# Second MLP over blocks of 512, 512, 512, 512 and 256 tokens in place of six blocks of 384

## The chip, the cores and the metric

The kernel runs on one core of a Trainium2 chip. The metric is the device time of one execution in microseconds (us); before the change it is 930.15 us, the median of three runs (930.00 to 930.42).

## What is computed

A sparse attention feeds two MLPs. With 2,304 tokens, 512 features and 2,048 hidden units, all in float32:

```
attn = softmax(mask(q @ k.T / 8)) @ v          # 4 batches, 8 heads, 576 positions
x  = attn as [2304, 512]
x2 = relu(x @ w1_in)**2 @ w1_out               # first MLP
h  = x2 @ w2_in                                # second MLP
y  = (h * sigmoid(1.702 * h)) @ w2_out
```

The weights arrive as float64 and are rebuilt as float32 on the chip ("decode").

## The kernel before

Every float32 product is made of three fp32r products: each operand is split into a high part and a low part (names ending in h and l), and high x high, low x high and high x low are summed in one PSUM bank.

The second MLP goes over the tokens in six blocks of 384, and within a block over 16 slices f of 128 hidden units. One such step, a **pass**, consists of

- `mm_h` (L340): 12 matmuls of 128x384, four input slices times three products, into one of the two banks tagged `h`. The weights are the stationary operand and the tokens (`xh`, `xl`) the moving one, so a matmul is as wide as the block.
- `act_sig`: ScalarE takes the sigmoid (L368), VectorE multiplies by h (L369), ScalarE rounds to the high part `gh` (L370), VectorE subtracts to get the low part `gl` (L371). Each of these is as wide as the block.
- `mm_acc2` (L395), called by `second`: for each token tile of 128 the stationary operand is a slice of `gh` or `gl` and the moving one is the output weights, 512 wide. With three token tiles there are nine matmuls of 128x512, three in each of three banks tagged `acc`. There are four such banks; the next block takes the next three in turn. A bank is summed over all 16 passes of its block and is then copied to SBUF and stored (`store_out`, L513).

The tokens of the next block are read back from DRAM (`load_x2`, L496 to L499) into a part of the ring `xh`, `xl` that holds 1,152 tokens. While the last block of the first MLP and the first block of the second run, VectorE and ScalarE still decode the weights of the second MLP: for each half slice VectorE does two TENSOR_SCALAR (L112, L114), two SCALAR_TENSOR_TENSOR (L119, L123) and one subtraction (L131), and ScalarE two operations (L110, L129).

The first MLP has blocks of 512, 256 and four times 384 tokens. Its `mm_h` is the same function; its second product, `mm_acc1` (L380), has the weights as stationary operand and `gh`, `gl` moving, so there both kinds of matmul are as wide as the block. Attention matmuls (L202, L223, L277, L301) are worked in between.

The order on each engine is set by a scheduler that simulates a timeline, except that TensorE's order in the first MLP and in the very last pass is that of the code.

Of the kernel before, what the change touches and what calls it, by code (L numbers as in the profile page):

```python
# [8 lines left out]
F32 = mybir.dt.float32  # L9
# [3 lines left out]
AF = mybir.ActivationFunctionType  # L13
ALU = mybir.AluOpType
# [7 lines left out]
def kernel(  # L22
# [20 lines left out]
    nc = tc.nc  # L43
    B, H, S, D = q.shape
    NT, DM = out.shape
    DFF = w1_in.shape[1]
    P = 128
    KC = DM // P
    NF = DFF // P

    NB2, NBMAX = 384, 512
    CUT1, CUT2 = [0, NBMAX, *range(768, NT + 1, 384)], [*range(0, NT + 1, NB2)]
    BLOCKS = [[(t0, t1 - t0) for t0, t1 in zip(cut, cut[1:])] for cut in (CUT1, CUT2)]
    N1, N2 = len(BLOCKS[0]), len(BLOCKS[1])
    RING = 2 * S
# [14 lines left out]
    def bank(tag):  # L70
        bufs = {"acc": 4, "h": 2, "att": 2}[tag]
        return psum.tile([P, 512], F32, tag=tag, name=f"ps_{tag}", bufs=bufs)

    xh = cpool.tile([P, KC, RING], F32R, name="xh")
    xl = cpool.tile([P, KC, RING], F32R, name="xl")
    x2d = dram.tile([P, KC, NT], F32, name="x2d")

    def f32(ap):
        return ap.bitcast(F32)
# [5 lines left out]
    marks = [None, None]  # L85
# [63 lines left out]
    def idle(ps, n):  # L149
        for _ in range(n):  # L150
            nc.tensor.matmul(ps, zeros[0][:, 0:P], zeros[0], start=True, stop=True)
# [175 lines left out]

    def mm_h(m, i, f, ph, ks, xl_last=False):
        ih, il = w_t[m, f][0:2]
        t0, nb = BLOCKS[m][i]  # L330
        c0 = t0 % RING
        prods = [(kk, w, x) for kk in ks for w, x in ((ih, xh), (il, xh), (ih, xl))]
        if xl_last:
            prods.sort(key=lambda p: p[2] is xl)
            idle(bank("h"), 4)
        for kk, w, x in prods:
            if xl_last and x is xl:
                idle(bank("h"), 3)
                xl_last = False
            nc.tensor.matmul(  # L340
                ph[:, 0:nb], w[:, kk * P:(kk + 1) * P], x[:, kk, c0:c0 + nb],
                start=(kk == KS[0] and w is ih and x is xh), stop=(kk == KS[-1] and x is xl),
            )
# [3 lines left out]
    def act_tiles(nb):  # L347
        return (
            gpool.tile([P, NBMAX], dt, tag=tag, name=tag, bufs=bufs)[:, 0:nb]
            for tag, dt, bufs in (("t", F32, 1), ("gh", F32R, 2), ("gl", F32R, 2))  # L350
        )
# [11 lines left out]
        nc.vector.tensor_tensor(out=gl, in0=t, in1=f32(gh), op=ALU.subtract)  # L363
        return gh, gl

    def act_sig(ph):
        t, gh, gl = act_tiles(NB2)
        marks[0] = nc.scalar.activation(t, ph[:, 0:NB2], AF.Sigmoid, scale=1.702)  # L368
        nc.vector.tensor_tensor(out=t, in0=ph[:, 0:NB2], in1=t, op=ALU.mult)  # L369
        marks[1] = nc.scalar.copy(gh, t)  # L370
        nc.vector.tensor_tensor(out=gl, in0=t, in1=f32(gh), op=ALU.subtract)  # L371
        return gh, gl
# [15 lines left out]
    def mm_acc2(f, g, acc, ts):  # L388
        _, _, oh, ol = w_t[1, f]
        gh, gl = g  # L390
        for lo, tt in ts:
            for t in tt:
                sl = slice(t * P, (t + 1) * P)
                for x, w in ((gl, oh),) if lo else ((gh, oh), (gh, ol)):
                    nc.tensor.matmul(  # L395
                        acc[t], x[:, sl], w,
                        start=(f == 0 and w is oh and not lo), stop=(f == NF - 1 and lo == 1),
                    )
# [81 lines left out]
    for word in FRONT.split():  # L480
        step, _, z = word.partition("+")
# [10 lines left out]
        fetch(0, n)  # L492

    def load_x2(i, c):
        s = lpool.tile([P, DM], F32, tag="tmp", name="tmp", bufs=6)[:, 0:NB2]
        nc.sync.dma_start(s, x2d[:, c, i * NB2:(i + 1) * NB2])  # L496
        c0 = i * NB2 % RING
        nc.scalar.copy(xh[:, c, c0:c0 + NB2], s)
        nc.vector.tensor_tensor(  # L499
            out=xl[:, c, c0:c0 + NB2], in0=s, in1=f32(xh[:, c, c0:c0 + NB2]), op=ALU.subtract,  # L500
        )

    def spill_x2(i, acc):
        pool, bufs = (lpool, 6) if lpool else (apool, 3)
        t0, nb = BLOCKS[0][i]
        for c in range(KC):
            s = pool.tile([P, DM], F32, tag="tmp", name="tmp", bufs=bufs)[:, 0:nb]
            (nc.scalar.copy if c % 2 else nc.vector.tensor_copy)(s, acc[c][:, 0:nb])  # L508
            nc.sync.dma_start(x2d[:, c, t0:t0 + nb], s)

    def store_out(i, t, acc):
        s = lpool.tile([P, DM], F32, tag="tmp", name="tmp", bufs=6)
        (nc.scalar.copy if t % 2 else nc.vector.tensor_copy)(s, acc)  # L513
        nc.sync.dma_start(out[i * NB2 + t * P:i * NB2 + (t + 1) * P, :], s)

    accs, gs = {}, {}

    def second(m, i, f):

        if f == 0:  # L520
            accs[m, i] = [bank("acc") for _ in range((KC, NB2 // P)[m])]
        acc, g = accs[m, i], gs.pop((m, i, f))
        if m == 0:
            mm_acc1(i, f, g, acc)
            if f == NF - 1:
                spill_x2(i, accs.pop((m, i)))
        elif i < N2 - 1 or f < NF - 1:
            mm_acc2(f, g, acc, [(0, range(3)), (1, range(3))])
            if f == NF - 1:
                for t in range(3):  # L530
                    store_out(i, t, acc[t])
        else:

            mm_acc2(f, g, acc, [(0, (0, 1)), (1, (0,))])
            store_out(i, 0, acc[0])
            mm_acc2(f, g, acc, [(1, (1,))])
            store_out(i, 1, acc[1])
            mm_acc2(f, g, acc, [(0, (2,)), (1, (2,))])
            for c0, copy, queue in ((0, nc.vector.tensor_copy, nc.sync), (DM // 2, nc.scalar.copy, nc.scalar)):
                s = lpool.tile([P, DM], F32, tag="tmp", name="tmp", bufs=6)[:, 0:DM // 2]  # L540
                copy(s, acc[2][:, c0:c0 + DM // 2])
                queue.dma_start(out[NT - P:NT, c0:c0 + DM // 2], s)

    gi = NPRO
# [3 lines left out]
    for i in range(N1):  # L548
        for f in range(NF):
            if i == N1 - 1 and f == 0:  # L550
                order.close()
                att.close()
                lpool = ctx.enter_context(tc.tile_pool(name="lpool", bufs=1, side="right", reuse_waits="tile"))
# [17 lines left out]
            if i == 0 and f == 0:  # L571
                ph = ph0.pop()
                mm_h(0, i, f, ph, KS[2:4], True)
            else:
                ph = bank("h")
# [23 lines left out]
    for i in range(N2):  # L599
        for f in range(NF):  # L600
            if i == 0:
                if f < 2:
                    fetch(1, 2 * (NF - 2 + f))
                    fetch(1, 2 * (NF - 2 + f) + 1)
                need(1, max(2 * f + 4, int(1.2 * (f + NF))), lpool, 6)
            if i == N2 - 1 and f == NF - 1:
                order.enter_context(tc.manual_schedule(engines={mybir.EngineType.PE}))
            ph = bank("h")
            mm_h(1, i, f, ph, KS)
            gs[1, i, f] = act_sig(ph)  # L610
            second(*prev)
            prev = (1, i, f)
            if 8 <= f < 8 + KC and i + 1 < N2:
                load_x2(i + 1, f - 8)
# [47 lines left out]
```

## Time and profile before

| | |
|---|---|
| median of three runs | 930.15 us |
| the profiled execution | 933.04 us, of it a span of 931.3 us on the core |
| TensorE matmul (PE) | 915.7 us busy, 98% of the span, 5739 matmuls |
| TensorE weight load (PEld) | 827.6 us, 89% |
| VectorE (DVE) | 491.1 us, 53% |
| ScalarE (ACT) | 410.1 us, 44% |
| granted TensorE clock | 0.995 of full speed over the span |

Matmuls overlap: the busy time of one runs past the start of the next, so what a matmul costs in a row is read from the distance between starts, not from its own duration.

### The profile page before, as it was taken

To read this page: it belongs to the slowest core of one execution; us is meant where nothing else is said; L and a number is where in the kernel's file an instruction comes from. 1 tells how busy PE (TensorE), PEld (TensorE's weight loads), DVE (VectorE), ACT (ScalarE), POOL (GpSimd) and SP (SyncE) were. 2 spreads that over 40 slices of the span, in tenths; PEclk is the share of its full clock that TensorE was granted. 3 is DMA by queue.
4 is the path that set the end of the run, shared out by engine and by line. 5 is a ranking of instruction groups with operands and counts; after the bars stand their busy time and mean duration, and the time that the engine had idled before them with its cause. 6 is when DMAs were issued, how large, how long until landed. Compare 5 with 4: busy or idle time off the path is not lost.

```text
span 931.3 us, 15027 instructions
## 1 busy us (share of the span) xinstructions
PE 915.7 (98%) x5739; PEld 827.6 (89%) x5739; DVE 491.1 (53%) x1335; ACT 410.1 (44%) x1123; POOL 2.9 (0%) x12
## 2 busy tenths in 40 slices
PE   8999999999999999999999999999999999999998
PEld 4677778899999999999999988899899999999897
DVE  4999996535563554532399998322322422322322
ACT  6977777425554544432355655322322322322222
POOL 0000000000000000000000000000000000000000
PEclk8999999999999999999999999999999999999999
DMA  8994111202210220100189501200200200100000
GB/s 203 325 343 134 32 32 33 72 1 61 62 44 14 85 63 12 36 1 1 59 268 299 198 11 34 69 1 0 68 1 1 69 1 1 60 1 1 34 1 34
DMA packets 72972, 64.34 MB, mean 69 GB/s; under 512 B 36708, under 2 KB 66116, under 8 KB 72900
## 3 DMA queue, kind: packets, MB, share of 16 engines
q1 hardware_dynamic: 72756, 63.25, 22.2%
q8 instruction: 45, 0.74, 0.3%
q14 instruction: 27, 0.22, 0.1%
q10 hardware_dynamic: 144, 0.13, 0.0%
HBM read 53.92 MB, written 9.44 MB: 68 GB/s over the span
## 4 chain that ended last, share of the span: by engine, by line
PE 85%; DVE 9%; ACT 2%; DMA 2%; issue 1%; SPq 0%; ACTq 0%; DVEq 0%
PE ps_h L340 39%; PE ps_acc L380 20%; PE ps_acc L395 19%; PE ps_h L301 2%; PE ps_att L223 2%; PE ps_att L202 1%; DVE tmp L119 1%; DVE whl L131 1%; PE ps_att L277 1%; DVE tmp L123 1%; DVE pr L239 1%; ACT pr L253 1%; DMA ld<-in_k_dram 1%; DVE pr L265 1%; DVE tmp L112 1%
## 5 line engine op out<-in xcount | busy, mean ns | idle before, releaser
L340 PE MATMUL ps_h<-xh,whl 128*128 128x384 f32 (+2 forms) x1528 | 394.8, 338 | 4.0 <-DVE whl L131 2.1
L340 PEld LDWEIGHTS ps_h<-xh,whl 128*128 128x128 f32 x1528 | 272.9, 188 | 19.1 <-DVE whl L131 2.7
L340 PE MATMUL ps_h<-xl,whl 128*128 128x384 f32 (+2 forms) x764 | 256.6, 336 | 0.0
L380 PE MATMUL ps_acc<-gh,whl 128*128 128x384 f32 (+2 forms) x768 | 153.1, 340 | 0.5 <-ACT tmp L508 0.5
L369 DVE TENSOR_TENSOR t<-ps_h,t 128x384 f32<-128x384 f32 x96 | 53.3, 556 | 187.7 <-ACT t L368 187.6
L395 PE MATMUL ps_acc<-whl,gh 128*128 128x512 f32 x576 | 150.7, 394 | 0.1
L340 PEld LDWEIGHTS ps_h<-xl,whl 128*128 128x128 f32 x764 | 143.7, 188 | 5.8
L368 ACT ACTIVATE t<-ps_h 128x384 f32<-128x384 f32 x96 | 47.2, 492 | 202.3 <-PE ps_h L340 192.4
L380 PEld LDWEIGHTS ps_acc<-gh,whl 128*128 128x128 f32 x768 | 128.3, 189 | 5.2 <-ACT tmp L508 0.7
L395 PEld LDWEIGHTS ps_acc<-whl,gh 128*128 128x128 f32 x576 | 106.6, 188 | 16.8 <-ACT tmp L508 0.5
L356 ACT ACTIVATE t<-ps_h 128x384 f32<-128x384 f32 (+2 forms) x95 | 46.1, 486 | 140.2 <-PE ps_h L340 132.8
L253 ACT ACTIVATE pr<-pr,st 72x72 f32<-72x72 f32 (+1 forms) x224 | 81.0, 365 | 23.3 <-DVE st L239 23.3
L362 DVE TENSOR_TENSOR t<-t 128x384 f32<-128x384 f32 (+1 forms) x80 | 42.3, 528 | 86.5 <-ACT gh L361 86.3
L395 PE MATMUL ps_acc<-whl,gl 128*128 128x512 f32 x288 | 83.7, 393 | 0.0
L380 PE MATMUL ps_acc<-gl,whl 128*128 128x384 f32 (+2 forms) x384 | 82.1, 335 | 0.0
L371 DVE TENSOR_TENSOR gl<-t,gh 128x384 fp32r<-128x384 f32 x96 | 53.4, 556 | 44.5 <-ACT gh L370 43.0
L370 ACT CAST gh<-t 128x384 fp32r<-128x384 f32 x96 | 49.2, 513 | 54.7 <-DVE t L369 53.1
L380 PEld LDWEIGHTS ps_acc<-gl,whl 128*128 128x128 f32 x384 | 66.1, 188 | 2.6
L395 PEld LDWEIGHTS ps_acc<-whl,gl 128*128 128x128 f32 x288 | 54.1, 188 | 12.5
L363 DVE TENSOR_TENSOR gl<-t,gh 128x384 fp32r<-128x384 f32 (+2 forms) x96 | 53.3, 556 | 8.8 <-ACT gh L359 4.4
L129 ACT CAST whl<-tmp 128x512 fp32r<-128x512 f32 x64 | 39.6, 620 | 16.4 <-DVE tmp L123 13.5
L110 ACT ACTIVATE tmp<-stg 128x512 f32<-128x512 f32 x64 | 42.8, 672 | 4.0 <-DMA stg<-in_moe_w_out_dram 1.9
(67 smaller groups left out, 720.8 us busy)
## 6 DMA issues: line engine op xcount, KB each, us to landing
stg<-in_moe_w_in_dram SPq DMA_DIRECT2D x32, 512.0 KB
stg<-in_moe_w_out_dram SPq DMA_DIRECT2D x32, 512.0 KB
tmp<-x2d SPq DMA_DIRECT2D x24, 192.0 KB
out_dram<-tmp SPq DMA_DIRECT2D x17, 256.0 KB
x2d<-tmp SPq DMA_DIRECT2D x16, 192.0 KB
ld<-in_k_dram SPq DMA_DIRECT2D x20, 128.0 KB
ldv<-in_v_dram SPq DMA_DIRECT2D x20, 128.0 KB
ld<-in_q_dram SPq DMA_DIRECT2D x16, 144.0 KB
```

The costliest lines, as they stand in the source:

```text
L110: nc.scalar.activation(t, high.bitcast(F32), AF.Abs)
L253: nc.scalar.activation(pr[0:R, i, j, 0:N], pr[0:R, i, j, 0:N], AF.Exp, bias=st[0:R, 0, x:x + 1], scale=-1.0, accum_out=st[0:R, 1, x:x + 1],)
L340: nc.tensor.matmul(ph[:, 0:nb], w[:, kk * P:(kk + 1) * P], x[:, kk, c0:c0 + nb], start=(kk == KS[0] and w is ih and x is xh), stop=(kk == ...
L356: marks[0] = nc.scalar.activation(t, ph[:, 0:nb], AF.Relu)
L362: nc.vector.tensor_tensor(out=t, in0=t, in1=t, op=ALU.mult)
L363: nc.vector.tensor_tensor(out=gl, in0=t, in1=f32(gh), op=ALU.subtract)
L368: marks[0] = nc.scalar.activation(t, ph[:, 0:NB2], AF.Sigmoid, scale=1.702)
L369: nc.vector.tensor_tensor(out=t, in0=ph[:, 0:NB2], in1=t, op=ALU.mult)
L370: marks[1] = nc.scalar.copy(gh, t)
L371: nc.vector.tensor_tensor(out=gl, in0=t, in1=f32(gh), op=ALU.subtract)
L380: nc.tensor.matmul(acc[c][:, 0:nb], w[:, c * P:(c + 1) * P], x, start=(f == 0 and w is oh and not lo), stop=(f == NF - 1 and lo == 1),)
L395: nc.tensor.matmul(acc[t], x[:, sl], w, start=(f == 0 and w is oh and not lo), stop=(f == NF - 1 and lo == 1),)
```

## The change

Block boundaries of the second MLP become 0, 512, 1024, 1536, 2048 and 2304. `mm_h` and `act_sig` take the width of their block, a block of 512 has four accumulators and the last one two, and the tokens of block i lie in the ring at 0 or 512 by turns. The last pass of the last block finishes its token tiles one after the other. The core of the diff:

```diff
-    NB2, NBMAX = 384, 512
-    CUT1, CUT2 = [0, NBMAX, *range(768, NT + 1, 384)], [*range(0, NT + 1, NB2)]
+    NBMAX = 512
+    CUT1, CUT2 = [0, NBMAX, *range(768, NT + 1, 384)], [*range(0, NT, NBMAX), NT]
...
     def mm_h(m, i, f, ph, ks, xl_last=False):
         ih, il = w_t[m, f][0:2]
-        t0, nb = BLOCKS[m][i]
-        c0 = t0 % RING
+        nb = BLOCKS[m][i][1]
+        c0 = i % 2 * NBMAX if m else BLOCKS[0][i][0] % RING
...
-    def act_sig(ph):
-        t, gh, gl = act_tiles(NB2)
-        marks[0] = nc.scalar.activation(t, ph[:, 0:NB2], AF.Sigmoid, scale=1.702)
-        nc.vector.tensor_tensor(out=t, in0=ph[:, 0:NB2], in1=t, op=ALU.mult)
+    def act_sig(ph, i):
+        nb = BLOCKS[1][i][1]
+        t, gh, gl = act_tiles(nb)
+        marks[0] = nc.scalar.activation(t, ph[:, 0:nb], AF.Sigmoid, scale=1.702)
+        nc.vector.tensor_tensor(out=t, in0=ph[:, 0:nb], in1=t, op=ALU.mult)
...
-            accs[m, i] = [bank("acc") for _ in range((KC, NB2 // P)[m])]
+            accs[m, i] = [bank("acc") for _ in range(BLOCKS[1][i][1] // P if m else KC)]
...
-            mm_acc2(f, g, acc, [(0, range(3)), (1, range(3))])
+            mm_acc2(f, g, acc, [(lo, range(len(acc))) for lo in range(2)])
             if f == NF - 1:
-                for t in range(3):
+                for t in range(len(acc)):
                     store_out(i, t, acc[t])
         else:
 
-            mm_acc2(f, g, acc, [(0, (0, 1)), (1, (0,))])
-            store_out(i, 0, acc[0])
-            mm_acc2(f, g, acc, [(1, (1,))])
-            store_out(i, 1, acc[1])
-            mm_acc2(f, g, acc, [(0, (2,)), (1, (2,))])
+            end = len(acc) - 1
+            mm_acc2(f, g, acc, [(lo, range(end)) for lo in range(2)])
+            for t in range(end):
+                store_out(i, t, acc[t])
+            mm_acc2(f, g, acc, [(0, (end,)), (1, (end,))])
```

`load_x2` and `store_out` use the block's own start and width in the same way. In the changed file the lines move: `mm_h` is L341 there and `mm_acc2` L397.

TensorE, inside a block. Before, from one group of nine accumulating matmuls to the next (gh is the high part, gl the low part of the activations):

```order
L395 MATMUL ps_acc<-whl,gh 128x512 x6
L395 MATMUL ps_acc<-whl,gl 128x512 x3
L340 MATMUL ps_h<-xl,whl 128x384
L340 MATMUL ps_h<-xh,whl 128x384 x2
L340 MATMUL ps_h<-xl,whl 128x384
L340 MATMUL ps_h<-xh,whl 128x384 x2
L340 MATMUL ps_h<-xl,whl 128x384
L340 MATMUL ps_h<-xh,whl 128x384 x2
L340 MATMUL ps_h<-xl,whl 128x384
L340 MATMUL ps_h<-xh,whl 128x384 x2
```

The same place inside a block of 512 now:

```order
L397 MATMUL ps_acc<-whl,gh 128x512 x8
L397 MATMUL ps_acc<-whl,gl 128x512 x4
L341 MATMUL ps_h<-xl,whl 128x512
L341 MATMUL ps_h<-xh,whl 128x512 x2
L341 MATMUL ps_h<-xl,whl 128x512
L341 MATMUL ps_h<-xh,whl 128x512 x2
L341 MATMUL ps_h<-xl,whl 128x512
L341 MATMUL ps_h<-xh,whl 128x512 x2
L341 MATMUL ps_h<-xl,whl 128x512
L341 MATMUL ps_h<-xh,whl 128x512 x2
```

Nine and twelve matmuls of two widths became twelve and twelve of one width.

TensorE, from block 0 to block 1, with buffer numbers. The accumulators of block 0 are ps_acc_6086 to 6089, those of block 1 ps_acc_6738 to 6741, in the same four banks. Now:

```order
L397 MATMUL ps_acc_6089<-whl_6507,gl_6657 128x512
L341 MATMUL ps_h_6718<-xl_73,whl_5414 128x512
L341 MATMUL ps_h_6718<-xh_72,whl_5414 128x512 x2
L341 MATMUL ps_h_6718<-xl_73,whl_5414 128x512
...
L341 MATMUL ps_h_6754<-xl_73,whl_5504 128x512
L397 MATMUL ps_acc_6738<-whl_5369,gh_6688 128x512 x2
L397 MATMUL ps_acc_6739<-whl_5369,gh_6688 128x512 x2
```

Between the last matmul into block 0's banks and the first into block 1's stand the last 7 matmuls of one `mm_h` (ps_h_6718) and all 12 of the next (ps_h_6754), 19 in all. Before, with one bank to spare, the first accumulating matmuls of block 1 stood closer and in two parts:

```order
L395 MATMUL ps_acc_6088<-whl_6476,gl_6614 128x512
L340 MATMUL ps_h_6666<-xh_72,whl_5414 128x384 x2
L340 MATMUL ps_h_6666<-xl_73,whl_5414 128x384
...
L340 MATMUL ps_h_6698<-xh_72,whl_5504 128x384 x2
L395 MATMUL ps_acc_6686<-whl_5369,gh_6642 128x512 x2
L340 MATMUL ps_h_6698<-xl_73,whl_5504 128x384
L395 MATMUL ps_acc_6686<-whl_5369,gl_6643 128x512
```

TensorE, the end of the program. Before:

```order
L340 MATMUL ps_h<-xl,whl 128x384
L395 MATMUL ps_acc<-whl,gh 128x512 x6
L395 MATMUL ps_acc<-whl,gl 128x512 x3
L395 MATMUL ps_acc<-whl,gh 128x512 x4
L395 MATMUL ps_acc<-whl,gl 128x512 x2
L395 MATMUL ps_acc<-whl,gh 128x512 x2
L395 MATMUL ps_acc<-whl,gl 128x512
```

And now:

```order
L341 MATMUL ps_h<-xl,whl 128x256
L397 MATMUL ps_acc<-whl,gh 128x512 x4
L397 MATMUL ps_acc<-whl,gl 128x512 x2
L397 MATMUL ps_acc<-whl,gh 128x512 x2
L397 MATMUL ps_acc<-whl,gl 128x512
L397 MATMUL ps_acc<-whl,gh 128x512 x2
L397 MATMUL ps_acc<-whl,gl 128x512
```

Between the last `mm_h` matmul and the first matmul on its own activations stand six matmuls where there were nine.

## Rows read from the trace of the kernel before

**Rows 1.** The page, busy time: us (share of the span) x instructions.
```profile
PE 915.7 (98%) x5739; PEld 827.6 (89%) x5739; DVE 491.1 (53%) x1335; ACT 410.1 (44%) x1123; POOL 2.9 (0%) x12
```

**Rows 2.** The page, the chain that ended last, share by line.
```profile
PE ps_h L340 39%; PE ps_acc L380 20%; PE ps_acc L395 19%; PE ps_h L301 2%; PE ps_att L223 2%; PE ps_att L202 1%; DVE tmp L119 1%; DVE whl L131 1%; PE ps_att L277 1%; DVE tmp L123 1%; DVE pr L239 1%; ACT pr L253 1%; DMA ld<-in_k_dram 1%; DVE pr L265 1%; DVE tmp L112 1%
```

**Rows 3.** Windows: length, busy PE, PEld, DVE, ACT, POOL (instructions), clock, DMA share, GB/s.
```profile
545.00:575.00 30.00, 29.85 (x150) 26.66 (x148) 30.00 (x62) 17.15 (x33) 0.00 (x0) 1.00 0.11 29
650.00:700.00 50.00, 50.00 (x252) 45.33 (x252) 16.54 (x30) 14.30 (x29) 0.00 (x0) 1.00 0.10 32
```

**Rows 4.** Timeline of TensorE, second MLP: start, duration (us), instructions, x count.
```profile
681.23 1.55 PE L395 MATMUL ps_acc<-whl,gh 128*128 128x512 f32 x6
...
708.43 0.33 PE L340 MATMUL ps_h<-xl,whl 128*128 128x384 f32 x1
...
709.50 0.33 PE L340 MATMUL ps_h<-xl,whl 128*128 128x384 f32 x1
...
710.54 1.55 PE L395 MATMUL ps_acc<-whl,gh 128*128 128x512 f32 x6
...
815.22 1.55 PE L395 MATMUL ps_acc<-whl,gh 128*128 128x512 f32 x6
```

**Rows 5.** Timeline of TensorE, first MLP, block of 512, twelve matmuls apart.
```profile
90.19 0.39 PE L340 MATMUL ps_h<-xl,whl 128*128 128x512 f32 x1
...
92.91 1.07 PE L380 MATMUL ps_acc<-gl,whl 128*128 128x512 f32 x4
```

**Rows 6.** Timeline of TensorE, first MLP, blocks of 384 and 256, twelve matmuls apart.
```profile
520.67 1.55 PE L380 MATMUL ps_acc<-gh,whl 128*128 128x384 f32 x8
...
522.75 0.51 PE L340 MATMUL ps_h<-xh,whl 128*128 128x384 f32 x2
...
178.81 1.12 PE L380 MATMUL ps_acc<-gh,whl 128*128 128x256 f32 x8
...
180.25 0.40 PE L340 MATMUL ps_h<-xh,whl 128*128 128x256 f32 x2
```

**Rows 7.** Timeline of TensorE, block of 512, right behind 16 attention matmuls.
```profile
95.15 0.40 PE L340 MATMUL ps_h<-xl,whl 128*128 128x512 f32 x1
...
96.08 0.61 PE L340 MATMUL ps_h<-xh,whl 128*128 128x512 f32 x2
```

**Rows 8.** Timeline of TensorE, first block of the second MLP; idle before and releaser in brackets.
```profile
535.34 0.86 PE L395 MATMUL ps_acc<-whl,gl 128*128 128x512 f32 x3
536.90 0.61 PE L340 MATMUL ps_h<-xh,whl 128*128 128x384 f32 x2 [0.70 <-DVE t L369]
```

**Rows 9.** Waits from 525 to 580 us: who for whom, us, times, longest.
```profile
PEld ps_h L340 <- DVE t L369: 2.3, 3, 1.1
```

**Rows 10.** VectorE's groups by shape, whole span: count | busy us, mean ns | idle before.
```profile
L371 DVE TENSOR_TENSOR gl<-t,gh 128x384 fp32r<-128x384 f32 x96 | 53.4, 556 | 44.5 <-ACT gh L370 43.0 <-PE ps_acc L395 1.1
...
L119 DVE SCALAR_TENSOR_TENSOR tmp<-stg,tmp 128x512 int32<-128x512 int32 x64 | 43.7, 685 | 0.6
...
L112 DVE TENSOR_SCALAR tmp<-tmp 128x512 f32<-128x512 f32 x64 | 26.8, 419 | 5.4 <-ACT tmp L110 5.1
...
L513 DVE COPY tmp<-ps_acc 128x512 f32<-128x512 f32 x11 | 7.1, 686 | 4.7 <-PE ps_acc L395 4.7
L363 DVE TENSOR_TENSOR gl<-t,gh 128x256 fp32r<-128x256 f32 x16 | 6.8, 425 | 1.3
```

**Rows 11.** ScalarE's groups by shape, whole span, columns as before.
```profile
L361 ACT ACTIVATE gh<-t 128x256 fp32r<-128x256 f32 x16 | 6.7, 419 | 0.4
...
L356 ACT ACTIVATE t<-ps_h 128x256 f32<-128x256 f32 x16 | 6.1, 380 | 25.6 <-PE ps_h L340 23.7 <-DVE gl L363 2.0
```

**Rows 12.** Timeline of all engines at the end.
```profile
922.48 0.35 PE L340 MATMUL ps_h<-xl,whl 128*128 128x384 f32 x1
...
922.87 0.49 ACT L368 ACTIVATE t<-ps_h 128x384 f32<-128x384 f32 x1 [2.56 <-PE ps_h L340]
...
924.75 1.09 PE L395 MATMUL ps_acc<-whl,gh 128*128 128x512 f32 x4
```

More of the change, by code (lines that the diff above doesn't have):

```diff
@@ L494, in load_x2 @@
     def load_x2(i, c):
[L495 to L498, printed above, removed]
+        t0, nb = BLOCKS[1][i]
+        s = lpool.tile([P, DM], F32, tag="tmp", name="tmp", bufs=6)[:, 0:nb]
+        nc.sync.dma_start(s, x2d[:, c, t0:t0 + nb])
+        c0 = i % 2 * NBMAX
+        nc.scalar.copy(xh[:, c, c0:c0 + nb], s)
         nc.vector.tensor_tensor(
-            out=xl[:, c, c0:c0 + NB2], in0=s, in1=f32(xh[:, c, c0:c0 + NB2]), op=ALU.subtract,
+            out=xl[:, c, c0:c0 + nb], in0=s, in1=f32(xh[:, c, c0:c0 + nb]), op=ALU.subtract,
         )
@@ L513, in store_out @@
         (nc.scalar.copy if t % 2 else nc.vector.tensor_copy)(s, acc)
-        nc.sync.dma_start(out[i * NB2 + t * P:i * NB2 + (t + 1) * P, :], s)
+        t0 = BLOCKS[1][i][0] + t * P
+        nc.sync.dma_start(out[t0:t0 + P, :], s)
     accs, gs = {}, {}
@@ L527, in second @@
         elif i < N2 - 1 or f < NF - 1:
-            mm_acc2(f, g, acc, [(0, range(3)), (1, range(3))])
+            mm_acc2(f, g, acc, [(lo, range(len(acc))) for lo in range(2)])
             if f == NF - 1:
-                for t in range(3):
+                for t in range(len(acc)):
                     store_out(i, t, acc[t])
         else:
-            mm_acc2(f, g, acc, [(0, (0, 1)), (1, (0,))])
-            store_out(i, 0, acc[0])
-            mm_acc2(f, g, acc, [(1, (1,))])
-            store_out(i, 1, acc[1])
-            mm_acc2(f, g, acc, [(0, (2,)), (1, (2,))])
+            end = len(acc) - 1
[3 more added lines that the diff above has]
+            mm_acc2(f, g, acc, [(0, (end,)), (1, (end,))])
             for c0, copy, queue in ((0, nc.vector.tensor_copy, nc.sync), (DM // 2, nc.scalar.copy, nc.scalar)):
                 s = lpool.tile([P, DM], F32, tag="tmp", name="tmp", bufs=6)[:, 0:DM // 2]
-                copy(s, acc[2][:, c0:c0 + DM // 2])
+                copy(s, acc[end][:, c0:c0 + DM // 2])
                 queue.dma_start(out[NT - P:NT, c0:c0 + DM // 2], s)
@@ L609 @@
             mm_h(1, i, f, ph, KS)
-            gs[1, i, f] = act_sig(ph)
+            gs[1, i, f] = act_sig(ph, i)
             second(*prev)
```

## The prediction

> **What bounds the kernel now.** I read the busy times first: TensorE is busy 98% of the span, VectorE 53%, ScalarE 44% [rows 1]. Busy time of overlapping matmuls proves little, so next the chain that ended last: its large pieces are the matmuls of `mm_h`, `mm_acc1` and `mm_acc2` (39, 20 and 19%), and nothing else has more than 2% [rows 2]. The windows then show what kind of bound it is: from 650 to 700 us TensorE works without a gap at the full clock, with VectorE and ScalarE at a third, while from 545 to 575 us, where weights are still decoded, VectorE is busy 30.00 of 30 us [rows 3]. So in the second MLP the time is the number of matmuls times their pace, and only near its start can another engine matter. A change that leaves the multiplications alone, as this one does, can gain only through the pace or through waits.
>
> **The pace.** It has to be read between starts. In the first MLP, long after the last change of shape, twelve matmuls take 2.72 us at 512 columns [rows 5], 2.08 us at 384 and 1.44 us at 256 [rows 6]: 226.7, 173.3 and 120.0 ns each. The steps from 256 to 384 and from 384 to 512 are both 53.3 ns for 128 columns, which leaves 13.3 ns per matmul that does not depend on its width. I call these the settled paces.
>
> The second MLP is slower than that. Equal places two blocks, 32 passes, apart lie at 681.23 and 815.22 us [rows 4], which is 4.187 us a pass (block borders included); at settled paces it would be 12 x 173.3 + 9 x 226.7 = 4,120 ns. The missing 67 ns lie behind the change of width: the first six `mm_h` matmuls behind a group of nine take 1.07 us, the six after them 1.04, which is settled [rows 4], and the nine take what is left, 4.187 - 2.11 = 2.08 us or 231 ns each. The same happens in the first MLP behind the narrow attention matmuls: four matmuls of 512 in 0.93 us, 232 ns each [rows 7], against 226.7 elsewhere in that block [rows 5]. There the two kinds of matmul are of one width, alternate just as often and use the same fresh `gh` and `gl`, yet stay settled. I take it that a change of width disturbs the pace for some ten matmuls and that this is the 67 ns.
>
> **The change part by part.**
>
> *Passes.* Before: 96 x 4.187 = 402.0 us. After: 64 passes of 24 matmuls of one width, 64 x 24 x 226.7 ns = 348.2 us, and 16 passes with 12 matmuls of 256 and 6 of 512, 16 x (1.440 + 1.360) = 44.8 us. In those 16 the width still changes. No row shows the cost of going between 256 and 512; it is bounded by nothing and by the 67 ns of a pass now, and since six of the nine wide matmuls remain I take 30 ns, 0.5 us together. So 393.5 us, a gain of 8.5 us. Of this 192 x 13.3 ns = 2.6 us come from the 192 `mm_h` matmuls that go away (960 in place of 1,152, with the same columns in all) and 5.9 from the width that no longer changes.
>
> The Trainium skill, page "TensorE: Matmul & The Clock Gate", section "Wait — 56ns, not 53.3ns?", gives a warm matmul N/2.4 + about 2.5 ns, of which only the 2.5 ns are per matmul. By that the 192 matmuls would be worth 0.5 us in place of 2.6. The rows have 13.3 ns at three widths [rows 5, 6], and the sum goes by them.
>
> *Waits while weights are decoded.* In the first block `mm_h` waits for a bank that VectorE has not yet read: three matmuls from 535.34 to 536.90 us take 1.56 us where 0.69 is usual, a loss of 0.87 [rows 8], and all weight loads waited 2.3 us in three places for this [rows 9], which bounds the loss from above because a matmul still runs meanwhile. A half slice costs VectorE 3 x 0.685 + 2 x 0.419 = 2.89 us (L119, its like L123 and L131; L112, its like L114) [rows 10]. The code asks for 1.2 halves a pass, 3.47 us, and `act_sig` adds 2 x 0.556 [rows 10]: 4.58 us in a pass of 4.19, or 109%. At 512 an operation is like the 512-wide copy, 0.686 [rows 10], so 3.47 + 1.37 = 4.84 in a pass of 5.44, or 89%. VectorE gets slack, but how the waits fall in its new order I cannot time. I take half of the loss between 0.87 and 2.3, a gain of 0.8 us; the ends are a gain of 2.3, and a loss of 2.1 if each of the three waits grows by one more decode operation of 0.685.
>
> *Block borders.* Four accumulators in four banks leave none free: the first matmul of a block must wait until the bank of the block before it is copied. It now stands 19 `mm_h` matmuls behind the last one of the old block (shown with the change), 19 x 226.7 ns = 4.3 us. Four copies of at most 0.686 [rows 10], two on VectorE and two on ScalarE, need 1.4 us. The cost is nothing. Without that cover it would be up to 1.4 us at each of four borders, 5.5 us; queued behind the copies are only the next `act_sig` and tokens for a later block.
>
> *Activations.* Inside a block of 512 they take at most 4 x 0.686 = 2.7 us [rows 10] and have 12 + 12 matmuls and more, over 5.4 us. In the block of 256: 0.380 + 0.425 + 0.419 + 0.425 = 1.65 us [rows 10, 11] against 6 + 12 matmuls, 2.8 us. Nothing is lost. The loads of tokens move the same bytes, and their buffer is free a block ahead.
>
> *The end.* The last `mm_h` matmul starts at 922.48, the sigmoid 0.39 later, and the first matmul on the result at 924.75, 1.88 behind the sigmoid [rows 12]; until then nine matmuls (2.08 us) fill the time, just enough. Now six do, 1.36 us and 0.12 for the `mm_h` matmul itself: 1.48. The chain shrinks too, to some 0.33 before the sigmoid (the 256-wide matmul is shorter) and 0.380 + 0.425 + 0.419 [rows 10, 11] plus the 0.3 us that hand-overs and the weight load take now (1.88 less operations of 0.49, 0.56 and 0.51): 1.85. A loss of 0.35 us, between nothing and 0.6. The stores behind it stay.
>
> *Sum.* -8.5 - 0.8 + 0.35 = -8.95 us. The profiled execution took 933.04, which gives 924.1. The median of the runs shown is 2.89 us below that execution, so the prediction is 930.15 - 8.95 = 921.2 us. With the ends of the terms (0.5 either way on the passes) it lies between 919.1 and 924.4.
>
> **The rivals.**
>
> *The slow pace does not come from the width.* It could belong to `mm_acc2` itself, whose stationary operand, unlike anywhere else, is `gh` and `gl`. For this speaks that the nine show no sign of settling within their group (231 ns on average), against it rows 7, where the weights are stationary and the pace suffers as well. If 67 ns a pass stayed, the passes would take 64 x 5.507 + 16 x 2.867 = 398.3, a gain of 3.7 and with the rest 4.15: 926.0 us. If all matmuls of 512 took 231 ns, 64 x 5.54 + 16 x 2.83 = 399.8: a gain of 2.2, with the rest 2.65, so 927.5 us.
>
> *Nothing changes.* If a matmul cost time by columns alone, the same columns would give the same time; then only the other terms remain and with them 929.7 us. The equal steps of 53.3 ns with 13.3 left over speak against it [rows 5, 6].
>
> *Slower: the banks.* The page "Perfetto Trace Analysis" of the Trainium skill, section "Matmuls" under "Optimizing Tensor Performance", wants independent groups to rotate through different banks, so that copying one overlaps the matmuls of the next; here that rotation ends. In this kernel the mechanism would be a copy that comes late on a queue. The wait starts when copies end more than 4.3 us behind the last matmul. At four borders and at the start of the second MLP, five in all, it outweighs the gain of 8.95 from 1.8 us each, that is with copies ending some 6.1 us behind; at 3 us each the time would be 936 us. Only decode work could delay them so, and it is over by the end of block 0; at the later borders VectorE and ScalarE are two thirds idle [rows 3]. For it speaks only the start of the second MLP.
>
> **How the numbers follow.** The settled pace for the blocks of 512 gets 0.67; the pace that stays slow 0.19 (926.0 to 927.5); no change 0.06; slower through late copies or the full VectorE queue 0.08. A difference of 0.2%, 1.9 us, is about what a measurement of this kernel can tell from none. The first two cases are faster by more than that, so faster 0.85, same 0.07, slower 0.08. The likeliest case has 919.1 to 924.4; to leave out no more than two in ten the range goes on into the second case: 918.8 to 926.8.
>
> **What would show it.** In the timeline, starts 0.227 us apart through whole passes of 512, with no slow matmuls behind the change from `mm_acc2` to `mm_h`, and places 16 passes apart in neighbouring blocks 87.0 us apart. TensorE's matmuls should fall by 192, to 5,547. The waits of `mm_h` for L369's successor should sum to less than 2.3 us, no wait of accumulating matmuls for the copies of `store_out` should appear, and one gap of a third of a microsecond before the last six matmuls. It is wrong if matmuls of 512 stay at 231 ns without a change of width, if each border shows a gap, or if VectorE falls behind through the whole first block.

## The result and the profile after

The changed kernel takes 919.71 us, the median of four runs (919.52 to 920.34). The kernel before, run beside it, took 930.28. The ratio is 0.9888 with a 95% interval of 0.9873 to 0.9902: 10.6 us less, where the forecast was 8.95 less and 921.2 us.

The page of after, busy time and the chain that ended last, beside [rows 1, 2]:

```profile
PE 904.4 (99%) x5539; PEld 792.5 (86%) x5547; DVE 486.3 (53%) x1297; ACT 404.8 (44%) x1089; POOL 2.9 (0%) x12
PE ps_h L341 42%; PE ps_acc L397 21%; PE ps_acc L382 20%; PE ps_h L302 2%; PE ps_att L224 2%; DMA stg<-in_moe_w_out_dram 2%; PE ps_att L203 2%; PE ps_att L278 1%; DMA stg<-in_moe_w_in_dram 1%; ACT pr L254 1%; PE ps_att L152 1%; DVE tmp L120 0%; DVE pr L240 0%; DVE whl L132 0%; PE ps_acc L224 0%
```

Weight loads went from 5739 to 5547, the 192 that the change takes away (eight matmul records are missing). The decode operations of VectorE (tmp L120 and whl L132), which had 1% each in [rows 2], are now at 0%: the chain runs through them less.

Three windows of after, columns as in [rows 3]:

```profile
545.00:575.00 30.00, 30.00 (x134) 24.85 (x133) 27.24 (x51) 15.06 (x27) 0.00 (x0) 1.00 0.12 36
650.00:700.00 50.00, 50.00 (x222) 41.39 (x222) 13.75 (x20) 12.06 (x20) 0.00 (x0) 1.00 0.01 5
```

While weights are decoded VectorE was busy 30.00 of 30 us; now it is 27.24, or 91%. In the 50 us from 650 TensorE works without a gap as it did, on 222 matmuls, all 512 wide, in place of 252 of two widths; the pace itself is read from starts.

The waits of before from 520 to 600 us hold, beside the row of [rows 9], one more of a weight load, at the start of the second MLP: the third accumulator of block 0 waits for ScalarE's copy (L508) out of a bank of the first MLP.

```profile
PEld ps_acc L395 <- ACT tmp L508: 0.5, 1, 0.5
```

In after no weight load waits in that time.

TensorE's timeline in after, from the first block's border to one block later:

```profile
611.29 0.39 PE L341 MATMUL ps_h<-xl,whl 128*128 128x512 f32 x1
...
615.37 0.39 PE L341 MATMUL ps_h<-xl,whl 128*128 128x512 f32 x1
615.60 1.98 PE L397 MATMUL ps_acc<-whl,gh 128*128 128x512 f32 x8
617.41 1.07 PE L397 MATMUL ps_acc<-whl,gl 128*128 128x512 f32 x4
618.32 0.62 PE L341 MATMUL ps_h<-xh,whl 128*128 128x512 f32 x2
...
702.64 1.98 PE L397 MATMUL ps_acc<-whl,gh 128*128 128x512 f32 x8
704.45 1.07 PE L397 MATMUL ps_acc<-whl,gl 128*128 128x512 f32 x4
705.36 0.62 PE L341 MATMUL ps_h<-xh,whl 128*128 128x512 f32 x2
```

Twelve accumulating matmuls take 615.60 to 618.32 = 2.72 us, 226.7 ns each, from the first one on. Sixteen passes, 615.60 to 702.64, take 87.04 us, 5.440 each: 24 x 226.7 ns and nothing else. Ahead of 615.60 stand the 19 `mm_h` matmuls at the border (611.29 to 615.60 = 4.31 us), and no row there has a bracket that names a copy.

A pass in the block of 256 (after, TensorE's timeline), where the width still changes:

```profile
894.39 1.09 PE L397 MATMUL ps_acc<-whl,gh 128*128 128x512 f32 x4
895.32 0.62 PE L397 MATMUL ps_acc<-whl,gl 128*128 128x512 f32 x2
895.78 0.40 PE L341 MATMUL ps_h<-xh,whl 128*128 128x256 f32 x2
```

Six accumulating matmuls take 1.39 us against 1.36 settled: 30 ns lost there. The narrow ones give some of it back (the order puts 18 of them behind this group), and a whole pass loses 18 to 20 ns, where the forecast had 30.

The end (after, timeline of all engines), beside [rows 12]:

```profile
910.95 1.09 PE L397 MATMUL ps_acc<-whl,gh 128*128 128x512 f32 x4
911.15 0.38 ACT L370 ACTIVATE t<-ps_h 128x256 f32<-128x256 f32 x1 [1.54 <-PE ps_h L341]
911.57 0.42 DVE L371 TENSOR_TENSOR t<-ps_h,t 128x256 f32<-128x256 f32 x1 [1.49 <-ACT t L370]
...
911.88 0.62 PE L397 MATMUL ps_acc<-whl,gl 128*128 128x512 f32 x2
912.03 0.41 ACT L372 CAST gh<-t 128x256 fp32r<-128x256 f32 x1 [0.49 <-DVE t L371]
...
912.49 0.30 PEld L397 LDWEIGHTS ps_acc<-whl,gh 128*128 128x128 f32 x2 [0.41 <-ACT gh L372]
912.49 0.73 PE L397 MATMUL ps_acc<-whl,gh 128*128 128x512 f32 x2
```

The six matmuls that fill the time last from 910.95 to about 912.3; the weight load for the last six waits until 912.49 for the rounding that began at 912.03. It stands idle for 0.41 us; since weight loads run ahead of matmuls, TensorE itself loses about 0.25. From the last matmul to the end of the span 4.14 us pass, where before had 4.68.

The profiled executions differ more, 933.04 against 919.69. Of those 13.35 us, 2.6 arise ahead of the MLPs, where the diff changes nothing, so they are no gain of the change: the first matmul of the first MLP into a bank `h` stands at 53.71 us before and 51.11 after. A window of before, then of after, shows one thing that differs there:

```profile
18.20:25.10 6.90, 6.62 (x43) 4.24 (x44) 3.45 (x8) 4.33 (x20) 0.00 (x0) 0.51 0.87 186
```

```profile
9.80:13.20 3.40, 3.18 (x14) 1.84 (x13) 0.00 (x0) 1.51 (x10) 0.00 (x0) 0.51 1.11 253
```

The granted clock stood at half, the 1.2 GHz level, for 6.9 us in one profiled execution and 3.4 in the other. TensorE had been busy 6.43 of 8.20 us ahead of it in the one and 3.36 of 4.80 in the other. I therefore compare from the first to the last matmul of `mm_acc2`: 528.99 to 926.59 = 397.60 us before, 528.56 to 913.76 = 385.20 after, 12.40 shorter. Of this 36 x 53.3 ns = 1.92 are not saved: the first three passes' `mm_h` matmuls, now wider, stand ahead of that stretch. That leaves 10.5 us, the size of the median's gain. The time from the first to the last matmul of `mm_acc2` is called its stretch below; what a run loses or gains elsewhere is not in it.

### The profile page after: what moved, and what is told of

Same layout as the page of the kernel before. It is cut to its first block, busy times and chain, and to the rows that moved or that the text cites. A ratio compares the mean times of both kernels' runs of the same rounds, so it can differ in the third digit from the quotient of the medians.

```text
span 917.9 us, 14535 instructions
## 1 busy us (share of the span) xinstructions
PE 904.4 (99%) x5539; PEld 792.5 (86%) x5547; DVE 486.3 (53%) x1297; ACT 404.8 (44%) x1089; POOL 2.9 (0%) x12
## 4 chain that ended last, share of the span: by engine, by line
PE 92%; DMA 3%; DVE 2%; ACT 2%; SPq 0%; issue 0%; ACTq 0%
PE ps_h L341 42%; PE ps_acc L397 21%; PE ps_acc L382 20%; PE ps_h L302 2%; PE ps_att L224 2%; DMA stg<-in_moe_w_out_dram 2%; PE ps_att L203 2%; PE ps_att L278 1%; DMA stg<-in_moe_w_in_dram 1%; ACT pr L254 1%; PE ps_att L152 1%; DVE tmp L120 0%; DVE pr L240 0%; DVE whl L132 0%; PE ps_acc L224 0%
## 5 line engine op out<-in xcount | busy, mean ns | idle before, releaser
L341 PE MATMUL ps_h<-xh,whl 128*128 128x512 f32 (+2 forms) x1400 | 378.6, 352 | 3.0 <-DVE whl L132 2.0
L341 PEld LDWEIGHTS ps_h<-xh,whl 128*128 128x128 f32 x1400 | 250.3, 188 | 32.7 <-DVE whl L132 2.7
L341 PE MATMUL ps_h<-xl,whl 128*128 128x512 f32 (+2 forms) x700 | 245.0, 350 | 0.0
L371 DVE TENSOR_TENSOR t<-ps_h,t 128x512 f32<-128x512 f32 (+1 forms) x80 | 51.0, 638 | 188.9 <-ACT t L370 188.9
L397 PE MATMUL ps_acc<-whl,gh 128*128 128x512 f32 x576 | 144.4, 390 | 0.0
L341 PEld LDWEIGHTS ps_h<-xl,whl 128*128 128x128 f32 x700 | 131.9, 188 | 12.6
L370 ACT ACTIVATE t<-ps_h 128x512 f32<-128x512 f32 (+1 forms) x80 | 44.4, 556 | 205.9 <-PE ps_h L341 197.9
L397 PEld LDWEIGHTS ps_acc<-whl,gh 128*128 128x128 f32 x576 | 107.0, 188 | 21.6 <-ACT gh L372 0.4
L397 PE MATMUL ps_acc<-whl,gl 128*128 128x512 f32 x288 | 78.6, 389 | 0.0
L373 DVE TENSOR_TENSOR gl<-t,gh 128x512 fp32r<-128x512 f32 (+1 forms) x80 | 51.1, 638 | 41.9 <-ACT gh L372 39.3
L372 ACT CAST gh<-t 128x512 fp32r<-128x512 f32 (+1 forms) x80 | 46.4, 580 | 48.8 <-DVE t L371 47.1
L397 PEld LDWEIGHTS ps_acc<-whl,gl 128*128 128x128 f32 x288 | 53.8, 188 | 11.3 <-DVE gl L373 0.2
L132 DVE TENSOR_TENSOR whl<-tmp,whl 128x512 fp32r<-128x512 f32 x64 | 43.9, 687 | 1.6 <-ACT whl L130 1.1
```

The lines of the kernel that those rows point to most:

```text
L132: nc.vector.tensor_tensor(out=lo, in0=t, in1=f32(hi), op=ALU.subtract)
L341: nc.tensor.matmul(ph[:, 0:nb], w[:, kk * P:(kk + 1) * P], x[:, kk, c0:c0 + nb], start=(kk == KS[0] and w is ih and x is xh), stop=(kk == ...
L370: marks[0] = nc.scalar.activation(t, ph[:, 0:nb], AF.Sigmoid, scale=1.702)
L371: nc.vector.tensor_tensor(out=t, in0=ph[:, 0:nb], in1=t, op=ALU.mult)
L397: nc.tensor.matmul(acc[t], x[:, sl], w, start=(f == 0 and w is oh and not lo), stop=(f == NF - 1 and lo == 1),)
```

## Experiments

The questions were whether the 67 ns a pass come from the change of width, as I held, or from `mm_acc2` and its stationary operand (the main rival); whether a matmul has 13.3 ns that do not depend on its width; what the waits in the first block are worth; and whether the borders cost nothing because the 19 matmuls cover the copies. The ratios are to the kernel before, run beside each group (930.69 us for E1 to E8, 931.33 for E9 to E11, 930.28 for the changed kernel itself), and as it moved by a microsecond between these groups, medians of different groups compare no better than that. Where no kernel is named, the edit is to the changed kernel.

### E1: `mm_h` 384 wide in blocks of 512

```diff
-        nb = BLOCKS[m][i][1]
+        nb = min(BLOCKS[m][i][1], 384) if m else BLOCKS[m][i][1]
...
-                sl = slice(t * P, (t + 1) * P)
+                sl = slice(t % 3 * P, (t % 3 + 1) * P)
```

`act_sig` gets the same width.

> The changed kernel, but in its blocks of 512 the first product computes 384 of the 512 token columns, the activations likewise, and the fourth token tile of the second product repeats the first one's activations: 128 tokens of each such block are left out. The number of matmuls stays (12 and 12 a pass), the two widths differ again. By columns and 13.3 ns a matmul a pass falls from 5.440 to 4.800 us, 64 of them by 41.0 us, to 878.7 us. Theory (a change of width disturbs the pace): each of these passes also loses 67 to 77 ns, 4.3 to 4.9 us together, so 883.0 to 883.6 us, with matmuls of 512 at about 231 ns. Rival (the slow pace belonged to the narrower second product with its high and low activations as stationary operand, or to three banks in place of four): the matmuls of 512 stay at 226.7 ns and the time is 878.7 us.

Measured: 883.29 us (881.80 to 884.32), ratio 0.9488 [0.9475, 0.9501]. The timeline of E1, TensorE, one pass:

```profile
701.78 2.01 PE L397 MATMUL ps_acc<-whl,gh 128*128 128x512 f32 x8
703.63 1.07 PE L397 MATMUL ps_acc<-whl,gl 128*128 128x512 f32 x4
704.54 0.33 PE L341 MATMUL ps_h<-xh,whl 128*128 128x384 f32 x1
...
706.65 2.01 PE L397 MATMUL ps_acc<-whl,gh 128*128 128x512 f32 x8
```

The same twelve accumulating matmuls now need 2.76 us instead of 2.72, and the pass 4.87 where settled paces give 12 x 173.3 + 12 x 226.7 ns = 4.80. With the change of width some 70 ns a pass come back (66 in the mean of such groups). The edit also lets the fourth token tile read the first one's activations and leaves out 128 tokens a block; the time lies where the change of width alone puts it.

### E2: every 512-wide `mm_h` matmul cut in two of 256

```diff
+            halves = (0, 256) if m and nb == NBMAX else (0,)
+            for a in halves:
+                e = a + nb // len(halves)
...
-                ph[:, 0:nb], w[:, kk * P:(kk + 1) * P], x[:, kk, c0:c0 + nb],
+                    ph[:, a:e], w[:, kk * P:(kk + 1) * P], x[:, kk, c0 + a:c0 + e],
```

> The changed kernel, with every matmul of 512 columns of the second MLP's first product cut in two of 256, same columns and weights: 768 matmuls more. Theory of 13.3 ns a matmul: 10.2 us, and 64 passes in which the width now changes between 256 and 512 at 18 to 30 ns each, 1.2 to 1.9 us: 931.1 to 931.8 us. Rival (about 2.5 ns a matmul, all else by columns): 1.9 us and the same change of width, 922.8 to 923.5 us.

Measured: 932.55 us (929.84 to 933.52), ratio 1.0015 [1.0005, 1.0025], which is 12.8 us above the median of the changed kernel, for 768 more matmuls with the same columns. The stretch of `mm_acc2`, with 732 of them, is 396.23 us long, 11.0 more than in after, so about 1.2 of the 12.8 lie outside it or between the groups of runs. One pass in E2's timeline of TensorE:

```profile
702.57 2.00 PE L400 MATMUL ps_acc<-whl,gh 128*128 128x512 f32 x8
704.41 1.07 PE L400 MATMUL ps_acc<-whl,gl 128*128 128x512 f32 x4
705.32 0.64 PE L344 MATMUL ps_h<-xh,whl 128*128 128x256 f32 x4
...
708.19 1.55 PE L400 MATMUL ps_acc<-whl,gh 128*128 128x512 f32 x6
```

Start to start it is 5.62 us against 5.440: 12 x 13.3 = 160 ns for the added matmuls and 20 for the change of width. The 24 of 256 take 2.87 us, 119.6 ns each, the pace of [rows 6]. The Trainium skill, page "TensorE: Matmul & The Clock Gate", section "Wait — 56ns, not 53.3ns?", has 2.5 ns per matmul; by an estimate from that the run would have ended at most 923.5. The measurement decides for 13.3 in this kernel.

### E5, E9: half as many changes of width in the kernel before

E9 lets blocks 1 to 5 of the kernel before run two `mm_h`, then two `mm_acc2` (nine and nine matmuls). That needs TensorE's order as in the code; E5 does this alone and is the control.

```diff
-            if i == N2 - 1 and f == NF - 1:
+            if i == 1 and f == 0:
                 order.enter_context(tc.manual_schedule(engines={mybir.EngineType.PE}))
```

> Control for the next kernel: the kernel before, with TensorE's order in the second MLP from its second block on as the code has it (12 matmuls of the first product, then the nine of the pass before). The change of width comes as often as before, so both theories expect the time of the kernel before, 930.3 us within 0.5.

Measured: 930.78 us (929.64 to 932.91), ratio 0.9999 [0.9989, 1.0009]. The order itself changes nothing. E9's further edit:

```diff
             mm_h(1, i, f, ph, KS)
+            late.append(prev)
+            flush = i == 0 or f % 2 == 0
+            if flush and len(late) == 2:
+                second(*late.pop(0))
             gs[1, i, f] = act_sig(ph)
-            second(*prev)
+            if flush:
+                second(*late.pop())
```

> The kernel with blocks of 384 and TensorE's order as the code has it from the second block on, again two passes together (24 matmuls of 384, then 18 of 512), but with the activations in the two buffers they had before: the second pass's activations are emitted behind the first pass's accumulating matmuls. In the earlier pairing the buffers had been moved to another place as well, and there 18 matmuls never settled. Theory (a change of width costs 66 ns, 38 in the nine matmuls of 512 behind it and 28 in the six of 384): the second nine of each 18 run at 226.7 ns and 40 changes fewer save 2.6 us against the control of 930.78: 928.2 us. Rival (the accumulating matmuls of 512 are slow as long as matmuls of 384 stand beside them, however long the group): all 18 near 231 to 234 ns, no gain, 930.8 us or a little more.

Measured: 927.68 us (927.05 to 929.12), ratio 0.9960 [0.9946, 0.9974], 3.1 us below the control's median; the stretch of `mm_acc2` is 395.19 us against 397.75 in E5, 2.56 shorter, which is the 2.6 that was expected. E9's timeline of TensorE:

```profile
702.79 1.55 PE L395 MATMUL ps_acc<-whl,gh 128*128 128x512 f32 x6
704.17 0.85 PE L395 MATMUL ps_acc<-whl,gl 128*128 128x512 f32 x3
704.87 1.52 PE L395 MATMUL ps_acc<-whl,gh 128*128 128x512 f32 x6
706.23 0.84 PE L395 MATMUL ps_acc<-whl,gl 128*128 128x512 f32 x3
706.91 0.51 PE L340 MATMUL ps_h<-xh,whl 128*128 128x384 f32 x2
```

The first nine take 2.08 us (231 ns each, as in [rows 4]), the second nine 2.04 (226.7). So accumulating matmuls do settle; in the kernel before, the group ended before they had. In the mean of E9's groups the first nine lose 41 ns together and the first six of 384 lose 26, 67 in all; the expectation's 38 and 28 were a little off in their shares.

### E6: the same pairing with the activations in other buffers

This was the first try at pairing. It differs from E9 in the order of `act_sig`, in where `t`, `gh` and `gl` lie and in the number of buffers of `gh` and `gl`, four in place of two.

```diff
-        t, gh, gl = act_tiles(NB2)
+        t, gh, gl = (
+            lpool.tile([P, NB2], dt, tag=tag, name=tag, bufs=bufs)
+            for tag, dt, bufs in (("t", F32, 1), ("gh", F32R, 4), ("gl", F32R, 4))
+        )
```

> The control with blocks of 384, two passes worked together from the second block on: 24 matmuls of 384, then 18 of 512, so the width changes half as often with the same matmuls (the activations have four buffers in place of two). Theory (each change of width costs some 67 ns until the pace has settled): 40 changes fewer in the 80 passes, 2.7 us, less up to 1.0 if 18 matmuls settle more slowly than nine: 1.7 to 2.7 us below the control, and the last matmuls of each group of 18 at 226.7 ns. Rival (the second product is slow by itself): the time of the control, all 18 at about 231 ns.

Measured: 931.76 us (930.96 to 932.88), ratio 1.0008 [0.9999, 1.0016]. My theory missed. E6's timeline of TensorE:

```profile
604.04 1.57 PE L398 MATMUL ps_acc<-whl,gh 128*128 128x512 f32 x6
605.45 0.86 PE L398 MATMUL ps_acc<-whl,gl 128*128 128x512 f32 x3
...
608.26 0.51 PE L340 MATMUL ps_h<-xh,whl 128*128 128x384 f32 x2
```

All 18 take 4.22 us, 234 ns each; they never settle. By this run alone the rival would have been right. But the passes of the first block, which are not paired, were also slower than in the kernel before, and what they shared with the rest was the buffers. E9 (pairing, old buffers) and E10 (other buffers, no pairing) part the two.

### E10: the changed kernel with only the buffers moved

```diff
-        t, gh, gl = act_tiles(nb)
+        t, gh, gl = (
+            lpool.tile([P, NBMAX], dt, tag=tag, name=tag, bufs=bufs)[:, 0:nb]
+            for tag, dt, bufs in (("t", F32, 1), ("gh", F32R, 2), ("gl", F32R, 2))
+        )
```

> The changed kernel with the activations of the second MLP (t, gh, gl) in buffers of the same size but in another pool, thus at another place in SBUF. Theory (the place of the stationary operand decides whether the accumulating matmuls settle, as the first pairing made it look): 864 accumulating matmuls lose up to 7 ns each, 6.0 us, so up to 925.7 us, with starts 231 to 234 ns apart. Rival (the place does not matter while all matmuls are 512 wide): 919.7 us and 226.7 ns.

Measured: 927.10 us (925.45 to 929.05), ratio 0.9960 [0.9944, 0.9976], 7.4 us above the changed kernel's median. E10's timeline of TensorE:

```profile
705.04 2.03 PE L400 MATMUL ps_acc<-whl,gh 128*128 128x512 f32 x8
706.91 1.10 PE L400 MATMUL ps_acc<-whl,gl 128*128 128x512 f32 x4
707.85 0.62 PE L341 MATMUL ps_h<-xh,whl 128*128 128x512 f32 x2
```

Twelve accumulating matmuls take 2.81 us, 234 ns each, with one width everywhere, while `mm_h` keeps its pace but for some 10 ns in the two behind each group. 864 of them by 7.4 ns are 6.4 us, and the stretch of `mm_acc2` is 391.65 us, 6.45 longer than in after. So the place of the buffers in SBUF can slow `mm_acc2`. The edit moves `t`, `gh` and `gl` together; that it is the place of the stationary operand is argued from this, that only the matmuls that load `gh` or `gl` slow down throughout. Which property of the place does it, the runs do not tell.

### E3, E4: a block of 384 first, or last

`CUT2` is `[0, 384, 896, 1408, 1920, NT]` in E3 and `[0, 512, 1024, 1536, 1920, NT]` in E4. Both have the same blocks; only E3 decodes weights during a block of 384.

> Second MLP in blocks of 384, 512, 512, 512 and 384. Passes: 48 x 5.440 + 32 x 4.187 = 395.1 us against 393.3 of the changed kernel, +1.8; the wait at the very end goes, -0.4. Theory on the waits of the first block (VectorE asked for 109% of a pass of 384 columns and for 89% of one of 512): they come back, +1.8, so 922.9 us, with weight loads of the first product waiting about 2.3 us for the multiplication on VectorE. Rival (they hung on the accident of one order): no waits, 921.1 us.

> Second MLP in blocks of 512, 512, 512, 384 and 384: the same passes as with 384 first, +1.8 and -0.4 at the end. Theory on the waits: none, since the first block is 512 wide: 921.1 us, 1.8 us below the kernel with 384 first. Rival: equal to that kernel.

Measured: E3 924.35 us (924.06 to 924.84), ratio 0.9931 [0.9919, 0.9944]; E4 923.14 (921.31 to 923.49), ratio 0.9913 [0.9900, 0.9927]. E3's waits from 520 to 600 us, the rows with a weight load for `mm_h`:

```profile
PEld ps_h L341 <- DVE t L371: 2.6, 2, 1.3
```

E4, like the changed kernel, has no wait of a weight load in that time. The place of the loss is shown. Its size can't be read from the two medians, which are 1.2 us apart where 1.8 were expected, with intervals of about 1.2 us each way: E4's slowest run lies 2 us above its fastest, 921.31, and its profiled execution lost 1.8 us more than after in the first MLP, which the edit leaves alone. The stretch of `mm_acc2` settles it: 391.43 us in E3 less the 1.92 by which 36 narrower matmuls ahead of it are shorter, against 386.79 in E4, a loss of 2.7. Of this 2.2 stand behind the two waits shown, the rest at two shorter ones of `mm_acc2`. E4's timeline in the first MLP:

```profile
160.28 4.63 SPq L512 DMA_DIRECT2D x2d<-tmp  x3
...
164.61 0.51 PE L382 MATMUL ps_acc<-gh,whl 128*128 128x256 f32 x2 [2.38 <-ACT tmp L511]
```

and the same place in after:

```profile
160.35 2.81 SPq L512 DMA_DIRECT2D x2d<-tmp  x3
...
162.87 0.50 PE L382 MATMUL ps_acc<-gh,whl 128*128 128x256 f32 x2 [0.56 <-ACT tmp L511]
```

### E7, E8: the border without its cover

E7 is the changed kernel with E5's edit (order as in the code from block 1 on), the control. E8 then puts the first `mm_acc2` of each later block, which is the first to use a bank again, ahead of the second pass's `mm_h`, so that it follows the old block's last `mm_acc2` at once:

```diff
+            early2 = i > 0 and f == 1
+            if early2:
+                second(*prev)
             ph = bank("h")
             mm_h(1, i, f, ph, KS)
             gs[1, i, f] = act_sig(ph, i)
-            second(*prev)
+            if not early2:
+                second(*prev)
```

> Control for the next kernel: the changed kernel, with TensorE's order from the second block on as the code has it. Twelve matmuls of the first product, 2.7 us, stand between the last of a block and the first of the next, and copying needs 1.4: 919.7 us within 0.5.

> The control with the first pass of a block's second product moved ahead of the next pass's first product: no matmul stands between the last into a bank and the first of the next block into the same bank, at four borders. Theory (the four of four banks are free because 12 to 19 matmuls cover the copies): a wait for the copies of 0.2 to 0.6 us at each border, since a bank is complete three matmuls before the end and the next needs them one after the other, and at most the 1.4 us of all copies: 0.8 to 2.4 us, at most 5.5, above the control, and waits of accumulating matmuls for the copies. Rival (the banks are freed in time without cover): the time of the control and no such wait.

Measured: E7 919.45 us (919.05 to 920.98), ratio 0.9874 [0.9860, 0.9889], the same as the changed kernel. E8 925.03 (923.76 to 926.88), ratio 0.9932 [0.9919, 0.9945], 5.6 us more than E7. E8's waits from 600 to 925 us:

```profile
PEld ps_acc L397 <- ACT gh L372: 3.1, 4, 1.1
...
PEld ps_acc L397 <- ACT tmp L516: 2.4, 4, 0.6
```

In E7 the first of these rows is a single wait of 0.4 us, the one at the end, and the second does not exist. With the cover gone each of the four borders waits for the copies of `store_out`: 0.6 us by the weight loads, 0.44 by the distances between TensorE's starts, 1.8 us together, within what was expected. So the banks are not free by themselves; the 19 matmuls hide them.

The other row is a side effect of the edit that I had not foreseen. E8's timeline, all engines, some microseconds behind the first border:

```profile
612.96 0.62 PE L341 MATMUL ps_h<-xh,whl 128*128 128x512 f32 x2
...
616.23 0.62 ACT L501 CAST xh<-tmp 128x512 fp32r<-128x512 f32 x1 [5.12 <-DMA tmp<-x2d]
...
616.76 0.59 ACT L370 ACTIVATE t<-ps_h 128x512 f32<-128x512 f32 x1
...
618.95 1.43 PE L397 MATMUL ps_acc<-whl,gh 128*128 128x512 f32 x5 [0.39 <-ACT gh L372]
```

With the first `mm_acc2` moved ahead, the second pass's activation has only the third pass's `mm_h` (2.72 us) to hide behind, where it otherwise has an `mm_acc2` as well; a copy of tokens (L501) that waits for its DMA stands ahead of it on ScalarE, and TensorE loses once more, 0.7, 1.0, 0.6 and 0.2 us at the four borders. From the first to the last matmul of `mm_acc2` E8 is 4.4 us longer than E7, 1.8 of it at the banks and 2.5 from this. The medians' other 1.2 us I can't place.

### E11: the block of 256 last but one

`CUT2` is `[0, 512, 1024, 1536, 1792, NT]`, so that the last pass has nine matmuls ahead of the last token tile again.

> The changed kernel with its block of 256 fourth and a block of 512 last. Theory (the last pass of a block of 256 has too few matmuls to cover its activations and waits 0.25 us net): the gap before the last matmuls goes, the rest stays, 919.3 to 919.6 us. Rival: nothing to tell, 919.7 us, or a new wait where the block of 256 meets the next one, a few tenths more.

Measured: 920.90 us (919.67 to 922.49), ratio 0.9888 [0.9870, 0.9907]. The gap is gone (first to last matmul of `mm_acc2` 384.91 us against 385.20), but from the last matmul to the end of the span 5.11 us pass where the changed kernel needs 4.14. E11's timeline at the end, TensorE and the DMA issues:

```profile
914.02 0.39 PE L397 MATMUL ps_acc<-whl,gl 128*128 128x512 f32 x1
914.03 1.31 SPq L518 DMA_DIRECT2D out_dram<-tmp  x3
...
915.43 0.41 SPq L546 DMA_DIRECT2D out_dram<-tmp  x1
```

The three stores of the other tiles now stand ahead of the last one on SP's queue. In this profile that is 0.7 us more in all; whether the medians show a loss can't be told from these runs. No version that I ran is clearly faster than the changed kernel.

## Why the prediction was right

*Direction and mechanism* held, and the measured time lies within the likeliest case's own range (its stated ends, 919.1 and 924.4, are a little narrow: the ends of the terms add up to 918.9 and 924.9). Term by term, measured against forecast, from the distances between starts beyond the settled pace:

- *Passes:* over the stretch of `mm_acc2` changes of width cost 6.33 us before and 0.37 after. With the 2.56 of the 192 matmuls that is a gain of 8.5, as forecast. The blocks of 512 came out as worked out; the 256-wide passes lost 18 to 20 ns in place of 30.
- *Decode waits:* this term was mis-sized. At the three waits of [rows 9] the kernel before loses 0.29 us at 531.2, 0.87 at 535.8 and 0.35 at 574.5, and 0.11 more in the matmul behind each: 1.84 us in all. After it there is none: TensorE is busy 30.00 of 30 us from 545 to 575 us, and no weight load waits between 520 and 600. The gain is 1.84, inside its ends but not the 0.8 that I took. I halved a loss on the ground that I could not time VectorE's new order. VectorE's demand, 89% forecast and 91% measured, stayed below its whole time, and all of the loss went; in E3, with 384 columns again, it is back.
- *The start of the second MLP:* the sum had no term for it. In before TensorE loses 0.27 us at 529.7, where it waits for a bank of the first MLP (the row of L508 above), and 0.11 in the matmul behind it. The changed kernel has no such wait, nor has any other run whose first block's `mm_h` covers 512 columns; E1, E3, E5 and E9, with 384 there, have it (E6, with other buffers, has not). The prediction thought of this place only as one where the change might lose.
- *Borders:* nothing, as forecast, and because of the cover, as E8 shows.
- *The end:* a loss of 0.25 against 0.35. But the stores behind it, which the prediction left as they were, got shorter: 4.14 us from the last matmul to the end in place of 4.68. Every run that ends on a block of 256 has 4.14 to 4.16 there and every one that ends on 384 has 4.63 to 4.68.

In the stretch of `mm_acc2` the sum is -8.5 - 1.84 - 0.38 + 0.25 = -10.5 us, as measured there; with the 0.54 behind it, 11.0, against 10.6 between the medians with an interval of about 1.4 each way. So the forecast of 8.95 came near with its largest term right, one too small by a microsecond and two left out.

*The cause of the 67 ns* was the step that carried most of the gain. Two runs with the old buffers agree that it is the change of width: E1 brings it back with the width, E9 saves half of it with half of the changes. Why a change of width costs this, no run shows.

*The main rival*, that `mm_acc2` is slow by its own stationary operand, fell in the form I gave it, since after runs at 226.7 ns from the first matmul on. But its idea is true elsewhere: in E6 and E10 the same operand at another place makes each such matmul 234 ns and no settling follows. My forecast rested on a condition that I did not know of, that `gh` and `gl` stay at a good place; that the change left their buffers as they were was luck. *Nothing changes* fell with E2: 768 matmuls without one more column cost 0.18 us a pass, 11.5 us in 64 passes, some 1.3 of it for the change of width. *Slower through the banks* did not happen. Its price without the cover is 0.44 us a border in E8, where the prediction named up to 1.4 as the bound.

## What to carry to other kernels

Read a matmul's price as the distance between starts, separately for each shape and behind each change of shape: here a loop that alternated 512 and 384 columns lost 67 ns per pair of changes, and each matmul cost 13.3 ns beside its columns, so equal widths of 512 won twice. All accumulator banks may be in use at once as long as enough other matmuls stand between the last use of a bank and its next; count them against the copies. When a wait comes from an engine at over 100% of its time, work out the engine's new demand: here it fell to 91% and the whole wait went.

## What the runs showed of the hardware

- Where the buffers lie in SBUF matters: moving three buffers of unchanged size, two of them the stationary operand of `mm_acc2`, took it from 226.7 to 234 ns a matmul and its stretch from 385.20 to 391.65 us (E10). Why is open.
- Behind a change from 384 to 512 columns the pace needs nine matmuls to settle, 41 ns in all, and from 512 to 384 six, 26 ns (E9); between 256 and 512 a pass loses only about 18 to 20 ns (after, E2).
- Parts that no edit touched moved the profiled time by some microseconds: 6.9 or 3.4 us at half clock early in the program (before, after), and stores of 2.81 or 4.63 us of issuing at 160 us (after, E4), which a copy of ScalarE and, behind it, TensorE wait for.
